# Block ring for u, joint turns, packed first values and a re-woven order in an attention-and-mixer kernel

## The chip, the core and the metric

The kernel runs on one core of one Trainium2 chip. The core has five engines, each with its own instruction queue: TensorE (PE: products, results in PSUM), VectorE (DVE), ScalarE (ACT), GpSimd (POOL, which also issues the loads that change the type) and SyncE (SP, which issues plain loads, the stores and the DMA transposes, here called turns). The metric is the time of one execution on the device, in microseconds. The kernel before takes 341.67 us, the median of 3 runs (340.97 to 342.67).

## The reference, cut to what matters

B = 8 batches, H = 8 heads, S = 576 tokens, 16 beacon keys, D = 64. Attention is causal over the tokens, and every token sees the beacons. Then come a low-rank mixing over tokens and a feed-forward part.

```python
scores = scale * np.matmul(q, k_all.transpose(0, 1, 3, 2))   # k_all: 16 beacons, then 576 tokens
scores = np.where(causal, -1000000000.0, scores)
a = np.exp(scores - scores.max(-1, keepdims=True)); a /= a.sum(-1, keepdims=True) + 1e-09
x = np.matmul(a, v_all)                                       # as (batch, token, 512)
h = x.transpose(0, 2, 1) @ U @ V                              # rank 32, over tokens
u = x + h.transpose(0, 2, 1)
out = u + np.maximum(u @ w_ch1, 0.0) @ w_ch2                  # 512 -> 2048 -> 512
```

## The kernel before

Attention works on pairs of heads, numbered 0 to 31: pair p is heads 2c and 2c + 1 of batch p // 4. Of a pair, q and k are loaded as rows, regrouped (`regroup`, tile `pr`) and turned into `qT` and `kT`. Pairs 0 to 11 are turned by PE products with the identity (`qkT_units`, tile `tps`); pairs 12 to 31 by a DMA transpose on SP (`turn_pair`, tile `raw`) and then put in token order by a copy (`order_units`). `score_units` makes the scores in four visits a to d (tile `sps`), each with two exponentials on ACT into `expt`; `mask_head` masks on DVE; `av_unit` multiplies with the values `vs`, in which column 65 of a head is one, and divides on DVE into `xb`.

Batch 0's q and k come as fp32 over SP and ACT's queues (`load_first`); every other load of q, k, v and the weights is on POOL's queue and changes to fp16 on the way. `v_loads` takes a beacon load and five loads of rows of 64 elements per batch or half batch.

`mix_units` makes u of a batch in a head and two parts of tokens, into `uT`, a ring of 3 x 512 tokens. For batches 0 to 2 x is brought in by products with the identity, from batch 3 on by turns of `xb` (`turn_x`, tile `xt`, one per 128 channels).

The feed-forward part works on nine blocks of 512 tokens of the flat batch-and-token axis (`block_steps`). For blocks 0 to 5, 16 units g make the hidden layer: four 512-column products each and the ReLU; for the lower half of the hidden layer the second 256 tokens are stored less the first 256, by one fused DVE instruction. Blocks 6 to 8 make the first layer by seven products F with sums (`first_product`, `first_sum`, `token_sum`). All blocks make the second layer by seven products P of sums (`operand_sum` p, `product`, `finish`), to which `finish` adds u, turned back to rows by SP (`turn`, tile `ut`, step U, one per 128 channels).

What sets the order is SCRIPT, a list of steps that is walked once: each step issues its instructions on its engines' queues, and each queue keeps that order. The letters: S a score visit, M a mask, A a product with values, G a regrouping, T a turned or reordered tile (with A, V or G for the engine ACT, DVE or POOL), R a DMA turn of a pair, X mixing, x a turn of x, k q b v loads, I a warm-up product, Z a tiny POOL copy that waits for a turn and so holds back the loads behind it. The tail after the bars is a guard on the sums of the softmax with a branch to a general path, which is not taken here.

Of the kernel before, what the change touches and what calls it, by code (L numbers as in the profile page):

```python
# [27 lines left out]
def kernel(  # L28
# [101 lines left out]
    Vsb = const.tile([P, S], F16, name="Vsb", tag="Vsb")  # L130
    ones = const.tile([P, 1], F16, name="ones", tag="ones")
# [4 lines left out]
    uT = const.tile([P, NCC, NBR * 512], F16, name="uT", tag="uT")  # L136
# [61 lines left out]
    def v_loads(src, bsrc, vs, hs):  # L198
        dst = vs[:, :].rearrange("p (c h e) -> p c h e", h=H, e=E)[:, :, hs, 0:D]
        beacon_load(nc.gpsimd, bsrc, dst[:, 0, :, :], hs)  # L200
        for j in range(NT):
            a = Nb if j == 0 else 0
            nc.gpsimd.dma_start(  # L203
                out=dst[a : a + nq[j], j, :, :], in_=src[hs, ds(q0[j], nq[j]), :].rearrange("h p d -> p h d")
            )

# [137 lines left out]
    def ring(t):  # L344

        return t % (NBR * 512)

    def turn_x(xb, xt, c):
# [3 lines left out]
            out=xt[:, c, :].rearrange("x (j p) -> x j p", p=P), in_=xb[:, c, :, :].rearrange("p j d -> p (j d)")  # L352
        )

    def mix_units(xb, u0, xt=None, shifted=True):
# [7 lines left out]
        edge = NBR * 512 - ring(u0)  # L363
        cuts = [0, edge if 64 <= edge < S else q0[2], S]
# [15 lines left out]
        def part(a, e):  # L380
            n = e - a
            ups = [pst([P, n], F32, name="ups") for _ in range(NCC)]
# [18 lines left out]
            for cc in range(NCC):  # L401
                dst = uT[:, cc, ds(ring(u0 + a), n)]
# [9 lines left out]
    def mlp_units(t0, n, dst):  # L412
# [4 lines left out]
        def g_unit(dc):  # L417
# [3 lines left out]
            for cc in range(NCC):  # L421
                nc.tensor.matmul(
                    g[:, 0:n], w1[:, cc, ts(dc, P)], uT[:, cc, ds(ring(t0), n)], start=(cc == 0), stop=(cc == NCC - 1)
# [8 lines left out]
        def c_unit(i, part):  # L432
# [10 lines left out]
            if part == 3:  # L443
                for cc in range(NCC):
                    nc.tensor.matmul(
                        ps[:m, ts(cc, P)], uT[:, cc, ds(ring(t0) + P * i, m)], ident, start=False, stop=True,
# [44 lines left out]
    def token_sum(t, i):  # L491

        H2 = 256
        x = uT[:, :, ds(ring(512 * t), 512)]
# [15 lines left out]
    def block_steps(t, dst):  # L510
# [6 lines left out]
        def turn(cc):  # L517
            if "u" not in cell:
                cell["u"] = utp.tile([P, 4, DM], F16, name="ut", tag="ut")
            nc.sync.dma_start_transpose(out=cell["u"][:, :, ts(cc, P)], in_=uT[:, cc, ds(ring(t0), 4 * P)])  # L520
            uses[t] += 1

        def g_unit(dc):
# [4 lines left out]
            for cc in range(NCC):  # L528
                nc.tensor.matmul(  # L529
                    g, w1[:, cc, ts(dc, P)], uT[:, cc, ds(ring(t0), 512)], start=(cc == 0), stop=(cc == NCC - 1)  # L530
                )
            if dc < NK:
                nc.scalar.activation(out=gT[:, dc, 0:H2], in_=g[:, 0:H2], func=AF.Relu)  # L533
                nc.vector.scalar_tensor_tensor(  # L534
                    out=gT[:, dc, H2:512], in0=g[:, H2:512], scalar=0.0, in1=gT[:, dc, 0:H2],
                    op0=ALU.max, op1=ALU.subtract,
                )
            else:
                nc.scalar.activation(out=gT[:, dc, :], in_=g, func=AF.Relu)  # L539
# [489 lines left out]
```

## Time and profile before

| | |
|---|---|
| median of 3 runs | 341.67 us |
| profiled execution | 341.91 us, span 340.3 us |
| busy: PE, DVE, ACT, POOL | 330.1, 263.4, 228.3, 103.6 us |
| granted TensorE clock, mean | 0.999 |
| chain that ended last | PE 84%, DVE 10%, issue 2%, ACT 1%, DMA 1% |
| DMA packets | 135600, 44.17 MB |

Busy times of engines overlap, so they don't add up to the span. A busy PE includes the warm-up products (tile `idle`, and some into `sps`): 44 of them in the first 36 us but for one. The chain is followed back from the last instruction; an engine's share of it says where the time went that nothing else hid. In a row of a group, the number behind the bar is the sum of busy us, then the mean ns of one instruction, then idle time of the engine just before it and who ended that. Line numbers are those of the kernel before.

### The profile page before, as it was taken

To read this page: it belongs to the slowest core of one execution; us is meant where nothing else is said; L and a number is where in the kernel's file an instruction comes from. 1 tells how busy PE (TensorE), PEld (TensorE's weight loads), DVE (VectorE), ACT (ScalarE), POOL (GpSimd) and SP (SyncE) were. 2 spreads that over 40 slices of the span, in tenths; PEclk is the share of its full clock that TensorE was granted. 3 is DMA by queue.
4 is the path that set the end of the run, shared out by engine and by line. 5 is a ranking of instruction groups with operands and counts; after the bars stand their busy time and mean duration, and the time that the engine had idled before them with its cause. 6 is when DMAs were issued, how large, how long until landed. Compare 5 with 4: busy or idle time off the path is not lost.

```text
span 340.3 us, 8963 instructions
## 1 busy us (share of the span) xinstructions
PE 330.1 (97%) x3527; PEld 227.9 (67%) x3527; DVE 263.4 (77%) x681; ACT 228.3 (67%) x495; POOL 103.6 (30%) x137
## 2 busy tenths in 40 slices
PE   6989999999999999999999999999999999999994
PEld 2456555684668755775577646765688888888883
DVE  3489687994869766984888768885999999896872
ACT  3779987849787889878886798267912842544500
POOL 7787673070530802360015220000001503303300
PEclk9999999999999999999999999999999999999999
DMA  8999999999999998999969998463445501203023
GB/s 170 237 188 167 126 184 197 118 127 213 159 163 189 163 203 127 128 148 191 183 95 145 175 174 115 33 161 99 48 63 159 85 13 63 77 3 94 3 80 128
DMA packets 135600, 44.17 MB, mean 130 GB/s; under 512 B 108384, under 2 KB 130912, under 8 KB 135552
## 3 DMA queue, kind: packets, MB, share of 16 engines
q0 software_dynamic: 69008, 17.54, 60.1%
q1 hardware_dynamic: 65952, 25.66, 39.9%
q8 instruction: 29, 0.48, 0.6%
q10 hardware_dynamic: 592, 0.34, 0.3%
q14 instruction: 19, 0.16, 0.2%
HBM read 37.63 MB, written 9.44 MB: 138 GB/s over the span
## 4 chain that ended last, share of the span: by engine, by line
PE 84%; DVE 10%; issue 2%; ACT 1%; DMA 1%; ACTq 0%; DVEq 0%
PE gps L529 25%; PE cpY L620 17%; PE cpD L620 9%; PE sps L316 8%; PE po L331 8%; PE cpA L620 4%; PE fpY L566 3%; DVE gT L581 3%; PE idle L241 2%; PE tps L263 2%; PE fpD L566 2%; DVE sT L601 1%; DVE ob L645 1%; DMA sth<-in_beacon_k_dram 1%; PE ups L397 1%
## 5 line engine op out<-in xcount | busy, mean ns | idle before, releaser
L321 ACT ACTIVATE expt<-sps 128x496 f16<-128x496 f32 (+2 forms) x256 | 111.6, 543 | 13.4 <-PE sps L316 11.9
L529 PE MATMUL gps<-uT,w 128*128 128x512 f16 x384 | 91.8, 380 | 0.0
L620 PEld LDWEIGHTS <-gT 128*128 128x128 f16 x576 | 54.6, 98 | 10.5 <-issue 2.3
L529 PEld LDWEIGHTS <-w 128*128 128x128 f16 x384 | 34.3, 98 | 37.1 <-issue 2.4
L587 POOL TENSOR_SCALAR gT<-gT 128x512 f16<-128x512 f16 x12 | 17.8, 1493 | 105.7 <-DVE gT L581 89.1
L620 PEld LDWEIGHTS <-sT 128*128 128x128 f16 x432 | 40.8, 98 | 8.0 <-issue 2.0
L203 POOL DMA_DIRECT2D vs<-in_v_dram x50 | 40.8, 838 | 3.8 <-DMA w<-in_moe_w_ch_dram 1.7
L304 DVE TENSOR_TENSOR expt<-expt,bigmask 128x512 f16<-128x512 f16 x64 | 26.9, 421 | 18.8 <-ACT expt L321 18.8
L331 PEld LDWEIGHTS <-expt 128*128 128x128 f16 (+1 forms) x960 | 35.2, 98 | 8.7 <-DVE expt L304 1.1
L539 ACT ACTIVATE gT<-gps 128x512 f16<-128x512 f32 x48 | 29.3, 618 | 15.4 <-PE gps L529 14.9
L331 PE MATMUL po<-vs,expt 128*128 128x65 f16 (+1 forms) x960 | 37.8, 194 | 0.7 <-DVE expt L304 0.6
L620 PE MATMUL cpY<-wsum,gT 128*128 128x256 f16 x288 | 36.1, 273 | 0.0
L620 PE MATMUL cpD<-w,sT 128*128 128x256 f16 x288 | 35.6, 273 | 0.3 <-DVE sT L601 0.3
L316 PE MATMUL sps<-qT,kT 64*128 64x80 f16 (+4 forms) x384 | 34.3, 284 | 0.2 <-DVE qT L265 0.2
L340 DVE TENSOR_TENSOR xb<-po,rec 128x320 f16<-128x320 f32 x64 | 31.5, 492 | 2.2
L534 DVE SCALAR_TENSOR_TENSOR gT<-gps,gT 128x256 f16<-128x256 f32 x48 | 19.7, 420 | 13.0 <-ACT gT L533 12.9
L109 ACT ACTIVATE hP<-fpY 128x512 f32<-128x512 f32 x24 | 13.7, 597 | 23.1 <-PE fpY L566 22.0
L533 ACT ACTIVATE gT<-gps 128x256 f16<-128x256 f32 x48 | 18.9, 412 | 12.2 <-PE gps L529 11.9
L316 PEld LDWEIGHTS <-kT 64*128 64x128 f16 x384 | 13.8, 94 | 19.8 <-issue 11.1
L645 DVE TENSOR_TENSOR ob<-cpY,ut 128x512 f32<-128x512 f32 (+1 forms) x28 | 18.7, 667 | 5.9 <-PE cpY L620 5.9
L566 PEld LDWEIGHTS <-wf 128*128 128x128 f16 x192 | 18.6, 98 | 3.1 <-issue 0.7
L620 PE MATMUL cpY<-w,gT 128*128 128x256 f16 x144 | 17.7, 273 | 0.0
(118 smaller groups left out, 484.7 us busy)
## 6 DMA issues: line engine op xcount, KB each, us to landing
out_dram<-ob SPq DMA_DIRECT2D x16, 512.0 KB, 4.7
st<-in_k_dram POOLq DMA_DIRECT2D x6, 512.0 KB, 8.0
st<-in_q_dram POOLq DMA_DIRECT2D x6, 512.0 KB, 8.3
vs<-in_v_dram POOLq DMA_DIRECT2D x18, 128.0 KB, 7.9
w<-in_moe_w_ch_dram POOLq DMA_DIRECT2D x4, 512.0 KB, 7.5
w<-in_moe_w_ch_dram POOLq DMA_DIRECT2D x2, 1024.0 KB, 12.0
stm<-in_k_dram SPq DMA_DIRECT2D x4, 256.0 KB, 6.0
out_dram<-ob SPq DMA_DIRECT2D x4, 256.0 KB, 2.8
```

The source lines that it names most:

```text
L203: nc.gpsimd.dma_start(out=dst[a : a + nq[j], j, :, :], in_=src[hs, ds(q0[j], nq[j]), :].rearrange("h p d -> p h d"))
L304: nc.vector.tensor_tensor(out=e4, in0=e4, in1=bigmask, op=ALU.min)
L316: nc.tensor.matmul(ps[i][:, ds(o, w)], kT[hp, c, ds(P * ch, P)], qT[hp, c, ds(qa, w)], start=True, stop=True,)
L321: nc.scalar.activation(out=ex[i][:, ds(PAD + SLOT * g, gw[g])], in_=ps[i][:, 0 : gw[g]], func=AF.Exp, scale=scale)
L331: nc.tensor.matmul(po[:, j, :], ex[0 : nk[c], ds(blk[(c, j)], P)], vs[0 : nk[c], ds(c * H * E + h * E, E)], start=(c == 0), stop=(c == j),)
L340: nc.vector.tensor_tensor(out=xb[:, h // 2, :, ds(D * (h % 2), D)], in0=po[:, :, 0:D], in1=r.broadcast_to([P, NT, D]), op=ALU.mult)
L529: nc.tensor.matmul(g, w1[:, cc, ts(dc, P)], uT[:, cc, ds(ring(t0), 512)], start=(cc == 0), stop=(cc == NCC - 1))
L534: nc.vector.scalar_tensor_tensor(out=gT[:, dc, H2:512], in0=g[:, H2:512], scalar=0.0, in1=gT[:, dc, 0:H2], op0=ALU.max, op1=ALU.subtract,)
L539: nc.scalar.activation(out=gT[:, dc, :], in_=g, func=AF.Relu)
L566: nc.tensor.matmul(ps[:, i, :], a[:, kk, ts(2 * mp + i, P)], b[:, kk, :], start=opens and i == 0 and kk == 0, stop=kk == 1, skip_group_che ...
L620: nc.tensor.matmul(ps[:, i, :], a[:, f, ds(P * i, P)], b[:, f, :], start=opens and i == 0 and f == 0, stop=f == NK - 1, skip_group_check=True,
L645: nc.vector.tensor_tensor(out=out, in0=ps[:, ii, :], in1=other, op=ALU.add)
```

## The change

1. `uT` is laid out by blocks: [P, 3, 4, 512] instead of [P, 4, 1536]. A batch's two parts of mixing are cut at the border of a block, 512 - 64 b tokens into batch b.
2. A turn of u and a turn of x take two groups of 128 channels each: 18 turns of u instead of 36, 10 of x instead of 20. `finish` reads the new layout of `ut`.
3. For blocks 0 to 5 the ReLU is one ACT instruction of full width; the difference of the token halves is taken in `operand_sum`, once per half of a block, for all nine blocks. The ReLU of 36 first products has a letter for its engine: 12 on POOL, 13 on DVE, 11 on ACT (before: 12 on POOL, 12 fused on DVE, 12 on ACT).
4. Batch 0's values are loaded with four tokens of a head in a row (tile `vf`, 116 partitions), and put in order by 16 products with a selection matrix `pick` (tile `vps`, steps D), copied to `vs` by ACT (2) and DVE (2).
5. SCRIPT is re-woven: 24 warm-up steps I instead of 37, 25 regroupings on POOL instead of 3, 20 of 40 reorderings of DMA-turned pairs on POOL instead of none.

```diff
-    uT = const.tile([P, NCC, NBR * 512], F16, name="uT", tag="uT")
+    uT = const.tile([P, NBR, NCC, 512], F16, name="uT", tag="uT")
...
+    def packed_loads(src, bsrc, vs, vf):
+        dst = vs[:, :].rearrange("p (c h e) -> p c h e", h=H, e=E)[:, 0, :, 0:D]
+        np_ = (S - nq[0]) // VJ
+        nc.gpsimd.dma_start(
+            out=vf[0:np_], in_=src[:, nq[0] : S, :].rearrange("h (p j) d -> p h (j d)", j=VJ)
+        )
+        nc.gpsimd.dma_start(out=dst[Nb : Nb + nq[0]], in_=src[:, 0 : nq[0], :].rearrange("h p d -> p h d"))
+        beacon_load(nc.gpsimd, bsrc, dst, ALLH)
+
+    def unpack(vf, vs, c, copy):
+        ps = pst([P, H, D], F32, name="vps")
+        n = nq[c]
+        rows = ds(VG * (c - 1), n // VJ)
+        for j in range(VJ):
+            nc.tensor.matmul(
+                ps[0:n], pick[rows, ds(VJ - 1 - j, n)], vf[rows, :, ds(D * j, D)], start=(j == 0), stop=(j == VJ - 1)
+            )
+        copy(out=vs[0:n, :].rearrange("p (c h e) -> p c h e", h=H, e=E)[:, c, :, 0:D], in_=ps[0:n])
...
-            out=xt[:, c, :].rearrange("x (j p) -> x j p", p=P), in_=xb[:, c, :, :].rearrange("p j d -> p (j d)")
+            out=xt[:, c : c + 2, :].rearrange("x c (j p) -> x (c j) p", p=P),
+            in_=xb[:, c : c + 2, :, :].rearrange("p c j d -> p (c j d)"),
...
-        edge = NBR * 512 - ring(u0)
-        cuts = [0, edge if 64 <= edge < S else q0[2], S]
+        cuts = [0, 512 - u0 % 512, S]
...
-            nc.sync.dma_start_transpose(out=cell["u"][:, :, ts(cc, P)], in_=uT[:, cc, ds(ring(t0), 4 * P)])
-            uses[t] += 1
+            nc.sync.dma_start_transpose(
+                out=cell["u"][:, cc : cc + 2, :, :].rearrange("x c j p -> x (c j) p"),
+                in_=ring(t0)[:, cc : cc + 2, :].rearrange("p c n -> p (c n)"),
+            )
+            uses[t] += 2
...
-            if dc < NK:
-                nc.scalar.activation(out=gT[:, dc, 0:H2], in_=g[:, 0:H2], func=AF.Relu)
-                nc.vector.scalar_tensor_tensor(
-                    out=gT[:, dc, H2:512], in0=g[:, H2:512], scalar=0.0, in1=gT[:, dc, 0:H2],
-                    op0=ALU.max, op1=ALU.subtract,
-                )
-            else:
-                nc.scalar.activation(out=gT[:, dc, :], in_=g, func=AF.Relu)
+            nc.scalar.activation(out=gT[:, dc, :], in_=g, func=AF.Relu)
...
-                if n == 3:
-                    nc.vector.scalar_tensor_tensor(
-                        out=n3, in0=n3, scalar=0.0, in1=a11, op0=ALU.max, op1=ALU.subtract
-                    )
-                elif n == 2:
-                    nc.gpsimd.tensor_scalar_max(out=out, in0=out, scalar1=0.0)
-                else:
-                    nc.scalar.activation(out=out, in_=out, func=AF.Relu)
+                RELU[eng](out)
...
+            if j == 0:
+                nc.vector.tensor_tensor(out=n3, in0=n3, in1=a11, op=ALU.subtract)
```

The order at three places. First ACT at the beginning, before; `sps` 225 and 226 are the two heads' scores of one visit, `st` is a tile of batch 1:

```order
L109 ACTIVATE pr<-stm 128x512
L109 ACTIVATE hd_142<-sth 80x128
L109 ACTIVATE qT<-tps 128x64
L109 ACTIVATE qT<-tps 128x512
L321 ACTIVATE expt_120<-sps_225 128x496
L321 ACTIVATE expt_121<-sps_226 128x496
L109 ACTIVATE pr<-st_191 128x512
L321 ACTIVATE expt_120<-sps_262 128x464
L321 ACTIVATE expt_121<-sps_263 128x464
L321 ACTIVATE expt_120<-sps_282 128x208
```

and after, from the first exponential on:

```order
L350 ACTIVATE expt_121<-sps_253 128x208
L350 ACTIVATE expt_122<-sps_254 128x208
L350 ACTIVATE expt_121<-sps_259 128x496
L350 ACTIVATE expt_122<-sps_260 128x496
L350 ACTIVATE expt_121<-sps_269 128x464
L350 ACTIVATE expt_122<-sps_270 128x464
L109 ACTIVATE kT_125<-tps 128x80
L109 ACTIVATE kT_125<-tps 128x512
L350 ACTIVATE expt_121<-sps_285 128x496
L350 ACTIVATE expt_122<-sps_286 128x496
L109 ACTIVATE vs_127<-vps 128x8x64
```

Three visits of pair 0 now follow each other, the regrouping of a later batch is gone from between them, and the unpacked values are copied here.

Second POOL at the beginning, before (`st` and `hd` are batch 1's k, `vs` batch 0's values):

```order
L196 DMA st_191<-in_k_dram 128x4x256
L190 DMA hd_189<-in_k_dram 64x4x64
L193 DMA hd_189<-in_beacon_k_dram 16x8x64
L193 DMA vs_126<-in_beacon_v_dram 16x4x64
L203 DMA vs_126<-in_v_dram 112x4x64
L203 DMA vs_126<-in_v_dram 128x4x64 x3
L203 DMA vs_126<-in_v_dram 80x4x64
L253 CAST pr<-stm 128x512
```

and after:

```order
L203 DMA hd_174<-in_beacon_k_dram 16x8x64
L220 DMA vf<-in_v_dram 116x8x256
L223 DMA vs_127<-in_v_dram 112x8x64
L203 DMA vs_127<-in_beacon_v_dram 16x8x64
L282 CAST pr<-stm 128x512
L780 CAST hd_142<-sth 80x128
L206 DMA st_177<-in_q_dram 128x4x256
L200 DMA hd_175<-in_q_dram 80x4x64
L206 DMA st_176<-in_k_dram 128x4x256
```

All of batch 0's values are now asked for ahead of batch 1's k and q, in three loads, where before one half came here and the other behind a slice of w1.

Third POOL in the middle, where batch 5's k is loaded, before (`gate` is the tiny copy of step Z):

```order
L196 DMA st_2119<-in_k_dram 128x8x256
L190 DMA hd_2117<-in_k_dram 64x8x64
L193 DMA hd_2554<-in_beacon_k_dram 16x8x64
L822 COPY gate_117<-raw 1x1
L196 DMA st_2557<-in_q_dram 128x8x256
L190 DMA hd_2555<-in_q_dram 80x8x64
```

and after:

```order
L865 COPY gate_118<-raw 1x1
L206 DMA st_2323<-in_k_dram 128x8x256
L200 DMA hd_2321<-in_k_dram 64x8x64
L206 DMA st_2324<-in_q_dram 128x8x256
L200 DMA hd_2322<-in_q_dram 80x8x64
L320 COPY qT<-raw 128x512 x2
L203 DMA hd_2321<-in_beacon_k_dram 16x8x64
L320 COPY kT_125<-raw 128x512
L865 COPY gate_118<-raw 1x1
L282 COPY pr<-st_2324 128x512
```

Before, only loads and the tiny copy stood here; now three reorderings of pairs 16 and 17 (`qT`, `kT`) and regroupings (`pr`) stand among the loads.

178 lines of the change are left out of this document (103 added, 75 removed).

## The prediction

> **What bounds the kernel now.** I read first the busy time by stretches, then the chain of work that ended last, then the instructions by group, and last the timeline of ScalarE (ACT) in the first 37 us. The stretches, with busy us and instructions per engine:
>
> ```profile
> 0.00:37.00 37.00, 32.53 (x356) 17.03 (x357) 24.17 (x95) 27.36 (x67) 27.80 (x51) 1.00 1.38 186
> 37.00:240.00 203.00, 202.97 (x2241) 130.48 (x2240) 155.50 (x426) 161.19 (x353) 58.03 (x74) 1.00 1.30 149
> 240.00:290.00 50.00, 49.19 (x525) 40.79 (x524) 47.83 (x103) 22.51 (x46) 8.98 (x6) 1.00 0.38 73
> ```
>
> The columns are PE, PE's weight loads, DVE, ACT, POOL, granted clock, DMA. After 37 us TensorE (PE) is busy without a hole for 203 us; in 240 to 290 DVE is nearly full too (47.83 of 50), and the chain runs there on DVE's sums; after that the chain is back on PE. Rows of the chain (start, us, what):
>
> ```profile
> 36.91 0.97 PE gps L529 x4
> ...
> 187.17 0.46 PE po L331 x15
> ...
> 195.42 3.45 PE gps L529 x16
> ...
> 269.95 2.50 DVE gT L581 x4
> ```
>
> Sixteen 512-column products in 3.45 us are 0.216 us each: in the dense part only fewer products or fewer seams between them could save anything, and the change removes no product. So there are three places to win or lose: the ramp up to the first feed-forward product at 36.91 us, the seams from 37 to 240, and the stage in which DVE is co-bound.
>
> **The ramp.** What holds it back is read on ACT, whose last bracket is its idle time before the row:
>
> ```profile
> 9.33 1.06 ACT L321 ACTIVATE expt<-sps 128x496 f16<-128x496 f32 x2 [1.09 <-PE sps L316]
> ...
> 11.71 1.00 ACT L321 ACTIVATE expt<-sps 128x464 f16<-128x464 f32 x2 [0.81 <-PE sps L316]
> 13.18 1.53 ACT L321 ACTIVATE expt<-sps 128x208 f16<-128x208 f32 x4 [0.46 <-PE sps L316]
> ...
> 25.30 1.06 ACT L321 ACTIVATE expt<-sps 128x496 f16<-128x496 f32 x2 [1.63 <-PE sps L316]
> ```
>
> ACT's work there, by the groups:
>
> ```profile
> L321 ACT ACTIVATE expt<-sps 128x496 f16<-128x496 f32 x128 | 68.1, 611 | 5.3 <-PE sps L316 4.6 <-ACT kT L109 0.6
> L321 ACT ACTIVATE expt<-sps 128x464 f16<-128x464 f32 x64 | 32.6, 577 | 3.6 <-PE sps L316 3.1 <-ACT gT L539 0.5
> L109 ACT ACTIVATE pr<-st 128x512 f16<-128x512 f16 x23 | 14.8, 652 | 4.3 <-DMA st<-in_k_dram 4.3
> L109 ACT ACTIVATE hP<-fpY 128x512 f32<-128x512 f32 x24 | 13.7, 597 | 23.1 <-PE fpY L566 22.0 <-ACT hP L109 0.7 <-DVE gT L581 0.2
> L109 ACT ACTIVATE kT<-tps 128x512 f16<-128x512 f16 x6 | 4.0, 664 | 0.0
> L109 ACT ACTIVATE kT<-tps 128x80 f16<-128x80 f16 x6 | 1.8, 296 | 1.0 <-PE tps L263 1.0
> L408 ACT ACTIVATE uT<-ups 128x336 f16<-128x336 f32 x4 | 1.6, 472 | 0.5 <-PE ups L397 0.5
> L109 ACT ACTIVATE Vsb<-vps 128x288 f16<-128x288 f32 x2 | 0.8, 532 | 0.0
> L408 ACT ACTIVATE uT<-ups 128x240 f16<-128x240 f32 x4 | 1.3, 368 | 0.0
> ```
>
> Up to the last write of u that the first product needs, ACT now has 42 exponentials, 5 turned pairs, 5 regroupings and a head copy, 2 spreads of V, 4 writes of u. After the change it has 44, 7, 2, none, none, 2, and 2 unpackings of values. Exponentials: four more of 464 and two fewer of 496, 4 x 0.577 - 2 x 0.611 = +1.09. Turns: 2 x (0.664 + 0.296) = +1.92. Regroupings: -3 x 0.652 = -1.96; the head copy counts as a 128x80 copy, -0.30. V: -1.06. Unpackings: 2 x 0.597 (the copy of as many fp32 elements out of PSUM) = +1.19. Writes of u: 2 x 0.597 - 2 x (0.472 + 0.368) = -0.49. Sum +0.4 us. DVE gives up three turns and takes two unpackings, the V spread and four small copies for the selection matrix; I count it as even. The unpacking's 16 products are 16 x 0.216 = 3.5 us of PE, and I cost them at nothing: PE is covered by its own warm-up products, of which the change drops 13 (13 x 0.216 = 2.8). If the cover is gone they cost up to 3.5.
>
> Against the +0.4 stand the waits. The first three rows wait because the four score groups of pair 0 are issued spread over other turns; afterwards three of them follow each other, so I take 1.4 of 1.09 + 0.81 + 0.46 = 2.36 us. The 1.63 at 25.30 I leave. Ramp: +0.4 - 1.4 = **-1.0**, bounds -3.6 (all four waits gone) and +3.9 (no wait gone, unpacking uncovered).
>
> **The loads of batch 0's values.** Twelve transfers become three. Landing times and the software queue as a whole:
>
> ```profile
> st<-in_k_dram POOLq DMA_DIRECT2D x6, 512.0 KB, 8.0
> vs<-in_v_dram POOLq DMA_DIRECT2D x18, 128.0 KB, 7.9
> ...
> q0 software_dynamic: 69008, 17.54, 60.1%
> ```
>
> Four times the bytes land in the same time when rows are long. The packed load has 116 x 8 x 256 x 2 bytes = 464 KB, so about 8 us after its issue at some 2.5 us: 10.5, when PE is at pair 0's scores. Counted at 0, since the unpacking stands behind those.
>
> **Joint turns.** 18 fewer turns of u and 10 of x.
>
> ```profile
> ut<-uT SPq DMA_TRANSPOSE x36, 3.8
> raw<-pr SPq DMA_TRANSPOSE x20, 4.6
> ...
> L520 SPq DMA_TRANSPOSE ut<-uT x36: 1189/1262/2685, 36.4 to 322.8; - x36
> ...
> L283 SPq DMA_TRANSPOSE raw<-pr x20: 1232/1266/3720, 83.0 to 223.4; - x20
> ```
>
> The turn raw<-pr already has eight 128-column blocks, as the joint turn of u will; u's has four now. Both hold SP 1.26 us, so the queue is freed of 28 x 1.26 = 35 us. Landing grows from 3.8 to 4.6; that of x, with ten blocks instead of five, to about 5 on the same slope. Who waits: the residual in `finish`, many products later, and the second part of a batch's mixing. For batch 7 six groups of eight and two of four 256-column products stand between the last turn of x and its use, 56 x 0.108 = 6.0 us, more than 5: cost 0, at worst the 5 - 3.8 = 1.2 once.
>
> **ReLU and differences.** For blocks 0 to 5 the half-width fused DVE instruction goes, ACT's ReLU is full width, and one bulk subtraction per half of a block comes:
>
> ```profile
> L534 DVE SCALAR_TENSOR_TENSOR gT<-gps,gT 128x256 f16<-128x256 f32 x48 | 19.7, 420 | 13.0 <-ACT gT L533 12.9
> L601 DVE TENSOR_TENSOR sT<-gT,sT 128x1024 f16<-128x1024 f16 x18 | 12.3, 683 | 0.2
> L583 DVE SCALAR_TENSOR_TENSOR gT<-gT 128x512 f16<-128x512 f16 x12 | 8.3, 692 | 1.5 <-DVE gT L581 0.5
> ...
> L533 ACT ACTIVATE gT<-gps 128x256 f16<-128x256 f32 x48 | 18.9, 412 | 12.2 <-PE gps L529 11.9
> L539 ACT ACTIVATE gT<-gps 128x512 f16<-128x512 f32 x48 | 29.3, 618 | 15.4 <-PE gps L529 14.9
> ```
>
> DVE: -19.7 + 12 x 0.683 = -11.5; ACT: 48 x 0.206 = +9.9. In blocks 6 to 8 DVE loses 12 x 0.692 = 8.3, gains 6 x 0.683 = 4.1 and 13 plain ReLUs; between the 0.335 and the 0.692 of the rows here and below that is 4.4 to 9, so about even in the co-bound stage. What DVE gains there is block 5's last fused instructions: half of 8 x 0.420 less 2 x 0.683, 1 us. I take **-0.5** for 240 to 290, bounds -2 and +1.
>
> **Work moved to POOL.** 20 of 40 reorderings of turned pairs and 22 more regroupings become POOL copies:
>
> ```profile
> L253 DVE COPY pr<-st 128x512 f16<-128x512 f16 x32 | 10.6, 335 | 0.0
> L291 DVE COPY kT<-raw 128x512 f16<-128x512 f16 x10 | 6.1, 606 | 0.8 <-DMA raw<-pr 0.8
> ...
> L587 POOL TENSOR_SCALAR gT<-gT 128x512 f16<-128x512 f16 x12 | 17.8, 1493 | 105.7 <-DVE gT L581 89.1 <-issue 16.5
> L196 POOL DMA_DIRECT2D st<-in_k_dram x8 | 7.1, 888 | 25.3 <-ACT kT L109 23.8 <-ACT expt L321 0.6 <-DMA w<-in_moe_w_ch_dram 0.5
> ...
> L190 POOL DMA_DIRECT2D hd<-in_k_dram x8 | 5.5, 684 | 0.0
> ...
> L253 POOL COPY pr<-st 128x512 f16<-128x512 f16 x1 | 0.6, 642 | 0.0
> ```
>
> POOL's reordering has no row. Its ends are 0.64 (the plain copy) and 1.49 (POOL's ReLU); scaled as DVE's, 0.642 x 606 / 335 = 1.16, which I take. ACT and DVE end some 5 and 15 us less loaded from 37 to 240, so that PSUM banks come free earlier and some seams close. No row prices a seam gone; the stretch's bounds are -3 and, POOL's copies late, +3. I take **-1.5**.
>
> Sum: 341.9 (the profiled execution; span 340.3, the rest lies around it; the median of the runs is 341.67) - 1.0 - 1.5 - 0.5, from the median: **338.7**.
>
> **Rivals.** (1) Nothing is gained: the exponentials and the loads set the ramp, PE's seams stay. ACT's sum of +0.4 speaks for it: 341.7. (2) More is gained, all waits of the ramp and both lower bounds in part: 335.5.
>
> (3) Slower: POOL is late. After the change the loads of batch 5's k and q stand on POOL, and behind them three reorderings and a beacon load, while PE has four g units, three groups of P and three A units to do before it needs pair 17: 4 x 0.864 + 3 x 0.864 + 3 x 0.46 = 7.4 us. The issues are 2 x (0.888 + 0.684) and at most 0.684 for the beacon, 3.8, so the copies may take 1.2 us each, hardly more than my 1.16. At 1.49 PE waits 0.9 us there; five such places give +4.5, less the gains: 345. A row shows how it could be worse:
>
> ```profile
> 5.77 0.23 DVE L741 CAST hd<-sth 80x128 f16<-80x128 f32 x1 [3.38 <-DMA sth<-in_beacon_k_dram]
> ...
> 20.53 1.16 DVE L741 CAST hd<-sth 80x128 f16<-80x128 f32 x1
> ```
>
> The same cast took 0.23 and 1.16 us, the second while POOL wrote a load of w1. The Trainium skill, SBUF — State Buffer, section "SBUF: two separate sides", says DVE and GpSimd share a port pair as an exclusive lock, held for a whole instruction; the trace agrees with it in that 0.9 us. By that rule 42 more POOL copies of 0.64 to 1.16 us could each hold up one DVE instruction, at an estimate some 20 us of DVE, which would eat the relief and make the seams' -1.5 a 0: 340.2.
>
> (4) Slower: the packed load runs on few DMA engines. All transfers of the trace have 128, 112, 80, 64, 32 or 16 partitions; this one has 116. A mean packet of the software queue is 0.601 x 340.3 x 16 / 69008 = 47 ns for 254 bytes; its 928 packets of 512 bytes are 47 to 94 ns. Over 16 engines that is 2.7 to 5.5 us, over four 11 to 22. In the second case it lands at 15 to 26 us instead of 10.5; PE stands in order at the unpacking, ACT has about 4 us of exponentials left: +3 to +10, 347. The Trainium skill, DMA: Bandwidth & Descriptors, section "Why a DMA increments its semaphore by 16 and not by 1", gives the rule: the largest divisor up to 16 of the slowest dimension, which for 116 is 4; and an exception in which the software queue uses ceil(partitions/16) per engine, 15 engines here. No run here shows which.
>
> **How the numbers follow.** Chances: forecast 0.40 (own range 336.5 to 340), more 0.12, nothing gained 0.22, POOL late 0.13, few engines 0.13. Half a per cent, 1.7 us, is about what a measurement of this kernel tells from no change. Faster: 0.12 and nearly all of 0.40, 0.50; same: 0.24; slower: 0.26. The range 334.5 to 345.5 leaves out half of the case of few engines and a tail below and above.
>
> **What would show it.** Right: the first feed-forward product at 35.5 to 36.5 us with ACT's early waits gone; the turn of u at 1.26 us on SP and 4.6 to landing; DVE some 15 us below 263; POOL's reordering near 1.1 us. Wrong: unpacking products that wait for the values' load, scores that wait for a POOL copy, or PE's stretch from the first product to the end not shorter than now.

## The result: slower by 5.6 %

The changed kernel takes 360.53 us, the median of 4 runs (359.48 to 361.86), against 341.32 us of the kernel before on the same chip (340.95 to 342.67). The ratio is 1.0557, with a 95 % interval of 1.0510 to 1.0604. The forecast was 338.7 with a range up to 345.5: wrong in sign and outside the range. A ratio leaves disturbed runs out (in experiment 1 the one of 351.09), so below it can differ from the quotient of the medians given beside it.

The profiled execution has a span of 358.7 us, 18.4 more than before. I read it in three stretches, by the first and the last start of the feed-forward products `gps` of blocks 0 to 5. Before, then after:

```profile
L529 PE MATMUL gps<-uT,w x384: 377/379/391, 36.8 to 242.1; 128*128 128x512 f16 x192
```

```profile
L563 PE MATMUL gps<-uT,w x384: 376/379/390, 49.8 to 260.4; 128*128 128x512 f16 x192
```

Up to the first product: 36.8 before, 49.8 after, +13.0. From the first to the last: 205.3 and 210.6, +5.3. From there to the end of the span: 98.2 and 98.3. So some 70 % of the loss is in the ramp, the rest in the middle, and the end is as long as it was.

**The ramp.** The tile of the packed values, with who waited for it, and how long its transfer took:

```profile
L231 PE MATMUL vps<-vf,pick x16: 577/626/645, 22.9 to 27.1; 32*128 32x512 f16 x12, 20*80 20x512 f16 x4
L220 POOL DMA_DIRECT2D vf<-in_v_dram x1: 1969/1969/1969, 2.6 to 2.6; - x1
...
  DVE vs L234: 13.7, 2
  ACT vs L109: 12.2, 2
  POOL hd L200: 12.1, 1
  PE vps L231: 10.2, 1
...
DMA to landing us min/median/max: 20.1/20.1/20.1
```

The load is issued at 2.6 us and its landing releases PE at 22.9, not at 10.5. PE, ACT, DVE and POOL all stand for it, between 10 and 14 us each. And the unpacking products take 577 to 645 ns each. By stretches (columns as in the prediction: PE, weight loads, DVE, ACT, POOL, clock, DMA share, GB/s):

```profile
12.00:15.00 3.00, 0.73 (x4) 0.10 (x2) 0.23 (x1) 2.14 (x6) 0.00 (x0) 1.00 1.36 215
15.00:18.00 3.00, 0.00 (x0) 0.00 (x0) 0.00 (x0) 0.00 (x0) 0.00 (x0) 0.55 1.34 227
18.00:21.00 3.00, 0.00 (x0) 0.00 (x0) 0.00 (x0) 0.00 (x0) 0.00 (x0) 0.50 1.12 153
...
26.00:30.00 4.00, 4.00 (x26) 1.74 (x23) 1.40 (x7) 2.47 (x6) 0.02 (x1) 0.50 1.02 144
30.00:35.00 5.00, 5.00 (x61) 2.98 (x59) 4.10 (x12) 3.26 (x9) 2.65 (x4) 0.76 0.28 34
```

None of these engines does anything from 15 to 21 us. The granted clock drops to one half while PE stands, and stays there until some way into 30 to 35 us, long after the work has come back: the shares of 0.55 and 0.76 put the drop at 15.3 us, 2.6 after PE's last product, and the return at 32.4. The Trainium skill, TensorE: Matmul & The Clock Gate, Part 1, puts that down to an activity window of about 3.4 us; the trace agrees as far as some three idle microseconds are enough to lose the clock, but here it took until past 30 us to get it back, over 9 us after PE had resumed.

**The middle.** The waits of PE:

```profile
PE vps L231 <- DMA vf<-in_v_dram: 10.2, 1, 10.2
PE po L360 <- DVE expt L333: 2.2, 4, 1.4
PE cpD L642 <- DVE sT L623: 1.8, 2, 1.6
```

Behind the load stand two waits for DVE, of 1.4 and 1.6 us at the longest. They end at 121.4 and 128.6 us. Ahead of the first, DVE and then POOL:

```profile
118.48 2.58 DVE L282 COPY pr<-st 128x512 f16<-128x512 f16 x1
120.98 0.41 DVE L333 TENSOR_TENSOR expt<-expt,bigmask 128x512 f16<-128x512 f16 x1
```

```profile
117.74 0.62 POOL L282 COPY pr<-st 128x512 f16<-128x512 f16 x1
118.29 1.07 POOL L320 COPY kT<-raw 128x512 f16<-128x512 f16 x1
119.30 1.05 POOL L320 COPY qT<-raw 128x512 f16<-128x512 f16 x1
120.30 0.60 POOL L282 COPY pr<-st 128x512 f16<-128x512 f16 x1
```

A DVE copy whose like takes 0.28 us lasts 2.58 us, as long as POOL copies one tile after another beside it. Ahead of the second, a sum that takes 0.68 us elsewhere takes 2.42 beside two more of POOL's copies:

```profile
126.14 2.42 DVE L623 TENSOR_TENSOR sT<-gT,sT 128x1024 f16<-128x1024 f16 x1
```

```profile
125.69 2.07 POOL L320 COPY qT<-raw 128x512 f16<-128x512 f16 x2
```

To compare kernels I use one sum below, DVE's *excess*: over all DVE instructions after 50 us that take over 0.1 us more than the median of their own line and shape, what they take above it. It is 1.2 us in 4 instructions before, 12.4 us in 20 after. By what POOL does beside them, some 9 of the 12.4 us stand beside its copies and some 3 beside its issues of loads; the 1.2 before stand mostly beside issues.

Some terms came out as forecast: POOL's reordering takes 1.10 to 1.14 us (estimate 1.16), and turns of x land in 5.0 (estimate 5).

### The profile page after: what moved, and what is told of

Its sections match the earlier page's. It is cut to its first block, busy times and chain, and to the rows that moved or that the text cites. A ratio compares the mean times of both kernels' runs of the same rounds, so it can differ in the third digit from the quotient of the medians.

```text
span 358.7 us, 8903 instructions
## 1 busy us (share of the span) xinstructions
PE 333.1 (93%) x3538; PEld 230.1 (64%) x3538; DVE 260.5 (73%) x640; ACT 220.5 (61%) x472; POOL 132.5 (37%) x171
## 4 chain that ended last, share of the span: by engine, by line
PE 68%; DVE 16%; ACT 6%; DMA 6%; issue 2%; POOL 0%; DVEq 0%; ACTq 0%; POOLq 0%
PE gps L563 17%; PE cpY L642 15%; PE cpD L642 9%; PE po L360 7%; DMA vf<-in_v_dram 6%; PE sps L345 5%; PE fpY L593 4%; ACT expt L350 4%; DVE sT L623 3%; PE cpA L642 3%; PE fpD L593 2%; ACT gT L566 2%; DVE xb L369 2%; DVE gT L608 2%; DVE expt L333 1%
## 5 line engine op out<-in xcount | busy, mean ns | idle before, releaser
L566 ACT ACTIVATE gT<-gps 128x512 f16<-128x512 f32 x96 | 56.0, 643 | 28.8 <-PE gps L563 28.2
L333 DVE TENSOR_TENSOR expt<-expt,bigmask 128x512 f16<-128x512 f16 x64 | 30.0, 469 | 25.7 <-ACT expt L350 25.6
L642 PEld LDWEIGHTS <-sT 128*128 128x128 f16 x432 | 41.0, 98 | 10.1 <-DVE sT L623 2.7
L213 POOL DMA_DIRECT2D vs<-in_v_dram x40 | 32.8, 833 | 4.3 <-DMA st<-in_k_dram 3.8
L282 POOL COPY pr<-st 128x512 f16<-128x512 f16 x22 | 14.1, 651 | 42.8 <-DMA raw<-pr 22.7
L345 PEld LDWEIGHTS <-kT 64*128 64x128 f16 x384 | 14.4, 96 | 20.1 <-issue 11.3
L320 POOL COPY qT<-raw 128x512 f16<-128x512 f16 x9 | 9.8, 1099 | 41.6 <-DMA raw<-pr 41.6
L320 POOL COPY kT<-raw 128x512 f16<-128x512 f16 x11 | 12.6, 1141 | 20.1 <-DMA raw<-pr 20.1
```

Source lines behind the costliest of these rows:

```text
L213: nc.gpsimd.dma_start(out=dst[a : a + nq[j], j, :, :], in_=src[hs, ds(q0[j], nq[j]), :].rearrange("h p d -> p h d"))
L320: copies[i](out=dst[:, c, w - 4 * P : w].rearrange("x (p j) -> x p j", j=4), in_=raw[:, i, :, :].rearrange("x j p -> x p j"),)
L333: nc.vector.tensor_tensor(out=e4, in0=e4, in1=bigmask, op=ALU.min)
L345: nc.tensor.matmul(ps[i][:, ds(o, w)], kT[hp, c, ds(P * ch, P)], qT[hp, c, ds(qa, w)], start=True, stop=True,)
L642: nc.tensor.matmul(ps[:, i, :], a[:, f, ds(P * i, P)], b[:, f, :], start=opens and i == 0 and f == 0, stop=f == NK - 1, skip_group_check=True,
```

## The experiments

Executions of the kernels that leave holes on PE scatter more than those of the kernel before (experiment 1 from 345.82 to 351.09 us, the kernel before beside it from 341.04 to 343.09). A hole may or may not cost clock: one of 2.0 us in experiment 12 is followed by 3.4 us at half clock, those of 1.4 and 1.6 us in the changed kernel's middle are not. Whether the scatter comes of that no run tests; I read the stretches beside the medians.

### 1. The packed load in two parts

```diff
-        np_ = (S - nq[0]) // VJ
-        nc.gpsimd.dma_start(
-            out=vf[0:np_], in_=src[:, nq[0] : S, :].rearrange("h (p j) d -> p h (j d)", j=VJ)
-        )
+        rest = src[:, nq[0] : S, :].rearrange("h (p j) d -> p h (j d)", j=VJ)
+        for p0, np_ in ((0, 112), (112, 4)):
+            nc.gpsimd.dma_start(out=vf[p0 : p0 + np_], in_=rest[p0 : p0 + np_])
```

> The changed kernel with its packed load of 116 partitions issued as two, of 112 and of 4 partitions; the same bytes to the same places, nothing else edited. Theory (few engines: with 116 partitions only four DMA engines carry the load, and everything queued behind it on those four waits too): the 112 partitions land at about 10 us instead of 22.7, PE's wait of 10.2 us at the unpacking goes, the granted clock stays 1.00, the first feed-forward product moves from 49.8 to about 37 us, and the time falls by about 13 to 347 (345 to 350), still above the kernel before. Rival (it is late by its amount or its place at the head of the queue): it lands after 18 us as now, and the time stays within 358 to 362.

Measured: 348.93 us (345.82 to 351.09), ratio 1.0133 (1.0088 to 1.0177). The two loads and the first product:

```profile
L230 PE MATMUL vps<-vf,pick x16: 372/374/406, 12.7 to 15.0; 32*128 32x512 f16 x12, 20*80 20x512 f16 x4
L221 POOL DMA_DIRECT2D vf<-in_v_dram x2: 601/720/840, 2.6 to 3.4; - x2
...
DMA to landing us min/median/max: 9.6/9.8/10.0
```

```profile
L562 PE MATMUL gps<-uT,w x384: 377/379/390, 38.2 to 250.3; 128*128 128x512 f16 x192
```

The first product starts at 38.2 instead of 49.8: 11.6 us are back, as many as the medians differ by (360.53 - 348.93 = 11.6). That these two agree so well is chance: the spans of the profiled executions differ by 10.1 us (358.7 and 348.6, the middle being 1.5 longer here), the ratios by 4.2 %, some 14 us. The rival that put the lateness down to amount or place falls, since both are unchanged. That it is the number of engines the trace shows in two more ways. The sixteen increments by which a load reports its parts done, for the 116-partition load and for the 112-partition one (us from the start):

```
116: 9.18 9.31 9.46 9.60 10.02 10.08 10.27 10.65 10.67 10.70 11.09 11.90 | 22.12 22.16 22.54 22.75
112: 8.07 8.13 8.17 8.71 8.83 9.03 9.04 9.24 9.27 9.29 9.30 10.24 10.40 11.62 12.02 12.59
```

I read this as twelve of sixteen engines with nothing to carry and four that carried it all. And the software queue's packets, after and in this run:

```profile
q0 software_dynamic: 68864, 17.55, 56.5%
```

```profile
q0 software_dynamic: 66192, 17.54, 56.8%
```

The same bytes in 2672 fewer packets. If four engines carry 116 x 8 / 4 = 232 packets each and every other engine runs through as many empty ones, that is 12 x 232 = 2784; less 12 x 8 for the four-partition load and 16 for the report of one load more, 2672 to the packet; the empty ones show as packets of 4 bytes, 2836 of them before 12 us after the change and 161 in this run.

### 2. Batch 0's values loaded as before

```diff
-    ... HqV0 I1 I1 f0 u ... Sa0:3 DA1 DV3 M0.1 q1A TqA1 I1 DA2 s DV4 Sc1 ... I1 w10 GqV5 ...
+    ... HqV0 I1 I1 v0A u ... Sa0:3 I4 I4 M0.1 q1A TqA1 I1 I4 s I4 Sc1 ... I1 w10 v0B GqV5 ...
```

> The changed kernel with batch 0's values loaded as before the change, in two halves by heads (the first at the place of the packed load, the second behind the load of w1's first quarter), and each of the four unpackings replaced by four warm-up products. Theory (few engines): time as with the packed load in two parts, 345 to 349, since both only take the late load away; first feed-forward product at 36 to 38 us. Rival (the re-woven order of the ramp is itself slow): the first feed-forward product stays beyond 42 us and the time above 352.

Measured: 350.38 us (348.16 to 351.23), ratio 1.0253 (1.0216 to 1.0290); first product at 40.7. Most of the lateness is gone here too, so the rival falls, but the time and the first product are both above what the theory said. By the ratios this kernel is over one per cent slower than experiment 1, and the intervals do not touch; the single times do overlap (348.16 to 351.23 against 345.82 to 351.09). Among PE's waits stands:

```profile
PE tps L292 <- POOL pr L282: 3.8, 1, 3.8
```

A regrouping that the new order gives to POOL stands behind the load issues of POOL's queue, of which there are twelve for batch 0's values instead of three. Under the new order the packed load is probably worth having, once it runs on all engines.

### 3. Warm-up products in the wait

```diff
-    ... Sa0:3 DA1 DV3 ...
+    ... Sa0:3 I48 DA1 DV3 ...
```

> The changed kernel with 48 more warm-up products of 512 columns (48 x 0.216 = 10.4 us) put ahead of the first unpacking on PE; their results are not used. They fill the wait for the load, which stays. Theory (the wait also costs clock: PE ran at half clock from 15.3 to 32.4 us because it stood still): granted clock 1.00 throughout, the 9.5 us of products done at half clock from 22.9 to 32.4 take 4.7, and the time falls by 3 to 5 us to 356 to 358. Rival (after the load has landed ACT and DVE set the pace of the ramp): within 1 us of 360.5 although the clock is 1.00.

Measured: 355.34 us (354.97 to 355.71), ratio 1.0390 (1.0350 to 1.0429). These are two runs, a gain of 5.2 us by the medians. The late load stays, the clock is 1.00:

```profile
12.00:23.00 11.00, 10.74 (x54) 4.77 (x53) 0.00 (x0) 2.11 (x6) 0.31 (x1) 1.00 1.10 168
23.00:33.00 10.00, 9.60 (x134) 5.58 (x130) 9.04 (x32) 9.03 (x24) 7.52 (x13) 1.00 0.95 134
```

```profile
L563 PE MATMUL gps<-uT,w x384: 376/379/390, 44.8 to 255.4; 128*128 128x512 f16 x192
```

The first product moves from 49.8 to 44.8: of the 11.6 us that the four engines cost, 5.0 are clock and 6.6 are waiting. Experiment 1's own ramp has 3.4 us at half clock, though; in experiments 4, 11 and 12, which have the same ramp, the clock stays whole and the first product comes at 36.6 to 36.8, by which the wait is 8 and the whole 13. DVE and ACT did not take up what the clock gave back; the rival falls.

### 4. POOL's copies given back to ACT and DVE

```diff
-    ... TkG13 ... TqG15 ... GkG18 ...
+    ... TkA13 ... TqV15 ... GkV18 ...   (all 20 reorderings, and the 16 regroupings of pairs from 12 on)
```

> As the kernel with the load in two parts, and besides all 20 reorderings of turned pairs that stood on POOL go back to ACT (11 of k) and DVE (9 of q), and the 16 regroupings of pairs from 12 on that stood on POOL go to DVE. Theory (a POOL copy holds up a DVE instruction for its whole length): DVE's single instructions of 2.58 us at 118.5 and 2.42 us at 126.1 take 0.28 and 0.68 again, PE's hole of 3.0 us between 120 and 140 closes, and the time falls by about 5 us against the kernel with the load in two parts, to 342 (340 to 344). Rival (the holes come of the order of the work or of the joint turns): the holes stay, and the time is within 1 us of the kernel with the load in two parts, or above it by the added work of ACT and DVE.

Measured: 366.88 us (364.70 to 367.77), ratio 1.0717 (1.0665 to 1.0770): 18 us slower than experiment 1 by the medians. Both expectations missed. DVE's excess did fall, from 12.0 to 3.2 us, but PE waits elsewhere:

```profile
PE gps L562 <- DVE uT L436: 9.0, 1, 9.0
PE po L359 <- DVE expt L332: 3.9, 1, 3.9
```

DVE stood still ahead of each:

```profile
138.36 0.50 DVE L281 COPY pr<-st 128x512 f16<-128x512 f16 x1 [9.74 <-DMA raw<-pr]
...
185.43 0.69 DVE L319 COPY qT<-raw 128x512 f16<-128x512 f16 x1 [4.41 <-DMA raw<-pr]
```

A regrouping has to wait until an earlier turn has read its buffer `pr`, a reordering until its turn has landed. In the changed kernel POOL spends 84 us on these two waits (22.7 for regroupings, 41.6 and 20.1 for reorderings of q and k), and PE's wait list shows 0.2 us behind it; on DVE, whose queue goes in order too, what PE needs next stands behind the wait. The order was written for POOL; this run doesn't price the hold-up.

### 5. Three of POOL's copies elsewhere

```diff
-    ... TkG14 ... TqG15 ... GkG18 ...
+    ... TkA14 ... TqA15 ... GkV18 ...
```

> The changed kernel with the load in two parts, and three of POOL's copies elsewhere: the reorderings of k of pair 14 and of q of pair 15 to ACT, the regrouping of k of pair 18 to DVE. In the kernel with the load in two parts POOL does these three in a row, and a DVE copy of 0.28 us that starts beside them at 107.2 us takes 3.5, while PE is busy only 16.98 of the 20 us from 100 to 120. Theory (the POOL copies hold DVE up, and that makes this hole): the DVE copy takes under 1 us, PE is busy over 19 of those 20 us, and the time falls by 2 to 5 us against the kernel with the load in two parts (348.9). Rival (ACT is full there, or what DVE does is not what PE waits for): the hole stays, time 347 to 351.

Measured: 349.10 us (346.93 to 351.40), ratio 1.0219 (1.0142 to 1.0295); the excess is 11.0 us. In experiment 1 there was

```profile
107.17 3.53 DVE L281 COPY pr<-st 128x512 f16<-128x512 f16 x1
```

Here the copy at 107 us takes 0.6 us and PE is busy 19.95 us from 100 to 120, as the theory has it; but from 120 to 140 it is busy only 17.41. DVE and POOL a little later:

```profile
115.28 2.45 DVE L334 TENSOR_TENSOR expt<-expt,mask 80x80 f16<-80x80 f16 x1
117.65 0.41 DVE L332 TENSOR_TENSOR expt<-expt,bigmask 128x512 f16<-128x512 f16 x1
```

```profile
115.58 2.08 POOL L319 COPY qT<-raw 128x512 f16<-128x512 f16 x2
```

A mask of 0.19 us takes 2.45, as long as the next two of POOL's copies. PE's holes from 120 to 140 are 0.92 and 0.22 us at 124.7, where experiment 4, without POOL's copies, has 0.93 and 0.21 before the same products, and 0.95 and 0.51 at 136.5, behind two masks that take 1.04 and 1.06 us beside a POOL copy. So the hold-up is real and moves to later copies, but only part of what PE loses here is its doing. The time stays where the rival had it.

### 6. The changed code under the old order

```diff
-    ... U0.0 ... U0.1 ... x12 ... x13 ... F62.3 F61.2 ... F63.3 ...
+    ... U0.0 ... x12 ... F62.3G F61.2 ... F63.3V ...   (order, loads and copies as before; each joint turn at its later place)
```

> The code of the changed kernel (ring of u by blocks, joint turns of u and x, full ReLU on ACT and differences in bulk) under the order of before: batch 0's values loaded as before, no unpacking, the copies on the engines that they had before; a joint turn stands where the later of its two single ones stood. Theory (these three parts cost nothing and gain little, the loss is the load and POOL): 340 to 342.5, POOL's part of DVE's delays gone. Rival (joint turns that land later, 4.2 and 5.0 us in place of 3.8 and 3.6, or the bulk difference ahead of the sums make PE wait): 343 to 347, with PE waiting on the second part of the mixing or on the sums of the cores.

Measured: 349.29 us (348.66 to 349.47), ratio 1.0219 (1.0170 to 1.0268). Both expectations are too low. POOL's part is gone as expected (excess 1.3 us), yet 7.5 us are lost: stretches of 36.9, 207.9 and 102.2 us against 36.8, 205.3 and 98.2.

### 7. POOL copies added to the kernel before

```diff
+        elif name == "J":
+            for i in range(2):
+                nc.gpsimd.tensor_copy(
+                    out=spare.rearrange("x (p j) -> x p j", j=2),
+                    in_=qT_of(int(arg) // NH2)[:, int(arg) % NH2, ds(S - 512 + 256 * i, 256)].rearrange(
+                        "x (j p) -> x p j", j=2
+                    ),
+                )
...
-    ... TqA12 ...
+    ... TqA12 J12 ...
```

> The kernel before with 40 POOL copies added, two behind each pair's reordering of q from pair 12 on, each from 256 columns of q in two-way order into a spare tile that nothing reads: no engine waits for them. Theory (a POOL copy holds up a DVE instruction that runs beside it, for its own length): DVE's time above the median of each instruction's own form after 50 us rises from 1.2 us to between 5 and 12, and the time by 1 to 4 us, to 343 to 346. Rival (the two engines do not disturb each other, and the long DVE instructions of the changed kernel come of something else): the excess stays below 2 us, and the time within 1 us of the kernel before.

Measured: 383.22 us (379.16 to 384.38), ratio 1.1181 (1.1092 to 1.1270). The excess is only 2.2 us, but:

```profile
PE po L332 <- DMA vs<-in_v_dram: 27.9, 14, 7.1
```

I had said that no engine waits for these copies. The loads behind them on POOL's queue do: a copy that waits for its q holds back the loads of later values, and PE stands for those. The run prices a mistake of mine, and shows how dear a POOL step is that waits.

### 8. POOL copies that wait for nothing

```diff
+        elif name == "J":
+            for i in range(int(arg)):
+                nc.gpsimd.tensor_copy(
+                    out=spare.rearrange("x (p j) -> x p j", j=2),
+                    in_=Vsb[:, ds(256 * (i % 2), 256)].rearrange("x (j p) -> x p j", j=2),
+                )
...
-    ... v3 ... q5 ...
+    ... v3 J4 ... q5 J4 ...   (behind 16 loads of later batches)
```

> The kernel before with 64 POOL copies of 256 columns in two-way order added, four in a row behind each of 16 loads of later batches, from the spread V (which is not written again) into a spare tile that nothing reads: unlike the copies of the earlier run they wait for nothing, so that no load is held behind one that waits. By that run's rows one takes 0.50 us, four some 2 us. Theory (while POOL's copies run in a row, a DVE instruction on half-precision data in SBUF waits for them): DVE's time above the median of each instruction's own form after 50 us rises from 1.2 us to between 5 and 15, and the time by 1 to 4 us, to 343 to 346. Rival (no such hold-up; the time of the earlier run came from the loads held behind the copies alone): excess below 2.5 us, time 341 to 342.5.

Measured: 343.50 us (342.99 to 345.11), ratio 1.0057 (1.0033 to 1.0080); excess 4.9 us in 20 instructions, against 1.2. So 64 copies make DVE 3.7 us longer and the kernel 1.7 to 2. This is the hold-up nearly by itself (the loads behind the copies start later too): real and small. The excess is just under the theory's 5, the time within its range. The single excesses are 0.14 to 0.27 us but for two of 0.41, which stand in the kernel before as well; all are less than one copy of 0.50. A DVE instruction got in between two of these copies. They write the same tile and stand 0.06 us apart in the trace, while the reorderings in a row start 0.05 to 0.08 us before the one ahead has ended; whether that is what makes the difference no run tried.

### 9. The same as 6, with ReLU and differences as before

```diff
-            nc.scalar.activation(out=gT[:, dc, :], in_=g, func=AF.Relu)
+            (ACT's half ReLU and DVE's fused instruction as before; no difference in operand_sum)
```

> The kernel with the changed code under the order of before, but with ReLU and differences as before: ACT's ReLU on half the columns and DVE's fused instruction for the other half, and DVE's fused difference in blocks 6 to 8. What is left of the change is the ring of u by blocks with the cuts of the mixing at its blocks, and the joint turns. Theory (the full ReLU on ACT and the differences in bulk cost the 7 us by which the changed code under the old order is slower): 341 to 343. Rival (the joint turns, which come later and land later, cost them): 346 to 350, with PE waiting behind the second parts of the mixing.

Measured: 343.79 us (343.07 to 344.86), ratio 1.0058 (1.0039 to 1.0077), between the two expectations. Ring, cuts and joint turns cost 0.6 %, 2.0 us; the other 5.5 us of experiment 6 are the full ReLU and the differences in bulk, under an order that does not fit them: 1.8 us in the middle (207.9 against 206.1) and 2.9 at the end (102.2 against 99.3). The ramps of the two profiled executions differ by 0.8 the other way.

### 10. Experiment 1 with the old ReLU in blocks 0 to 5

The `g_unit` of the kernel before, and the bulk difference only for blocks 6 to 8:

```diff
-            if j == 0:
+            if j == 0 and t > 5:
```

> The changed kernel with the load in two parts, and in blocks 0 to 5 ReLU and difference as before the change (ACT on half the columns, DVE's fused instruction on the other half; no bulk subtraction there). The order stays the re-woven one, with POOL's copies. Theory (ReLU and differences in bulk cost the stretch from the first to the last feed-forward product of blocks 0 to 5 some 2 us, as under the old order, where it went from 206.1 to 207.9): 345 to 347.5, that stretch 2 us or more shorter than the 212.1 of the kernel with the load in two parts. Rival (under the new order ACT has room for the full ReLU, and DVE, held up by POOL, has none for the fused instructions): 350 or more.

Measured: 354.93 us (351.93 to 356.40), ratio 1.0373 (1.0307 to 1.0440), 6 us slower than experiment 1 by the medians, 8 by the ratios; its middle stretch is 218.2 us instead of 212.1. The rival is right. Going back to the old ReLU gained 5.5 us under the old order and loses 6 here (in blocks 0 to 5 alone).

### 11. POOL's reorderings in halves

```diff
+            n = 2 if copies[i] == nc.gpsimd.tensor_copy else 1
+            m = P // n
+            for s in range(n):   (tokens ds(m * s, m) each)
```

> The changed kernel with the load in two parts, and each of POOL's 20 reorderings of a turned pair (1.1 us) cut into two copies of half the tokens. The same bytes, the same engines and order. Theory (DVE waits for the POOL copy that is running, and can start between two: beside copies of 0.50 us the longest excess was 0.25 to 0.27 us on the masks and sums): DVE's time above the median of its forms falls from 12.0 us to about half, no DVE instruction takes over 1.5 us, PE's hole of 3.0 us between 100 and 140 shrinks to under 1.5, and the time falls to 345 to 347. Rival (DVE waits until POOL pauses, however the copies are cut): single DVE instructions of 2 us and more stay, and so does the hole; time 347 to 350.

Measured: 347.71 us (346.44 to 348.62), ratio 1.0171 (1.0135 to 1.0207): not told apart from experiment 1. The excess falls to 8.9 us, less than hoped, and one DVE copy at 105.2 us still takes 2.4 us too long; PE is busy 17.57 of the 20 us from 100 to 120. At the place that matters DVE waited for the whole row of copies, however they were cut, as the rival had it.

### 12. Two reorderings on POOL exchanged

```diff
-    ... TkG15 X2.1 b6 GqG17 ... TkG14 Sc14 ...
+    ... TkG14 X2.1 b6 GqG17 ... TkG15 Sc14 ...
```

> The changed kernel with the load in two parts, and two reorderings on POOL exchanged in the order: that of k of pair 14 stands where that of pair 15 stood, and the other way round. In the kernel with the load in two parts POOL stands still for 3.72 us before 105.86, waiting for the turn of pair 15, with the reordering of pair 14 queued behind it; then four copies run in a row, PE waits 1.20 us for pair 14's k, and a DVE copy takes 3.53 us beside them, after which PE waits 1.43 us more. Theory (POOL's queue is late there, and its copies in a row hold DVE): both of PE's waits go or fall below 0.5 us, PE is busy over 19 of the 20 us from 100 to 120, and the time falls by 2 to 4 us, to 345 to 347. Rival (the hold-up comes again at the next run of POOL's copies, as where three copies were taken off POOL): PE's loss in 100 to 140 stays 2.5 us or more, time 347.5 to 350.

Measured: 347.10 us (345.18 to 348.52), ratio 1.0138 (1.0086 to 1.0191). Both aimed-at waits are gone, and in their place:

```profile
112.29 2.88 DVE L622 TENSOR_TENSOR sT<-gT,sT 128x1024 f16<-128x1024 f16 x1
```

```profile
112.55 2.06 POOL L319 COPY qT<-raw 128x512 f16<-128x512 f16 x2
114.53 0.54 POOL L203 DMA_DIRECT2D hd<-in_beacon_k_dram  x1
```

```profile
PE cpD L641 <- DVE sT L622: 2.0, 1, 2.0
```

PE loses 3.3 us from 100 to 140 (36.67 busy of 40), as the rival had it, though the time lies between the two expectations: the hold-up moves to a sum of 0.68 us, which takes 2.20 longer, about as long as two copies.

The kernels side by side, us (profiled executions):

| kernel | to the first product | first to last | to the end |
|---|---|---|---|
| before | 36.8 | 205.3 | 98.2 |
| after | 49.8 | 210.6 | 98.3 |
| 1 load in two parts | 38.2 | 212.1 | 98.3 |
| 2 old loads | 40.7 | 207.3 | 98.5 |
| 3 warm-up in the wait | 44.8 | 210.6 | 98.3 |
| 4 no POOL copies | 36.8 | 229.9 | 98.1 |
| 5 three copies off POOL | 38.7 | 208.6 | 99.2 |
| 6 old order | 36.9 | 207.9 | 102.2 |
| 7 before, waiting POOL copies | 36.2 | 247.0 | 98.4 |
| 8 before, free POOL copies | 35.9 | 207.5 | 98.2 |
| 9 old order, old ReLU | 37.7 | 206.1 | 99.3 |
| 10 as 1, old ReLU | 35.6 | 218.2 | 98.3 |
| 11 short POOL copies | 36.6 | 210.2 | 98.5 |
| 12 exchange | 36.8 | 210.4 | 98.3 |

No kernel here is faster than the one before.

## Why the prediction was wrong, point by point

**The packed load, "Counted at 0".** This is the step that failed. It took the landing of loads with other shapes, "about 8 us after its issue at some 2.5 us: 10.5", for one of 116 partitions. What happened is rival 4, to which I gave 0.13: four engines, landing at 22.7 inside its 15 to 26. Its price of 3 to 10 us was too small all the same: 11.6 by experiment 1 and more by others, since it counted the wait (6.6 to 8) and not the clock that PE loses while it stands (5.0, experiment 3). The rows said enough to give this rival more than 0.13: no transfer of the trace had such a shape, and on four engines the same packet times gave 11 us and more. The rule of the Trainium skill, DMA: Bandwidth & Descriptors, section "Why a DMA increments its semaphore by 16 and not by 1", the largest divisor up to 16, gives 4 for 116 and 16 for 112. Both agree with the increments; the exception that I set against it did not apply here.

**The ramp, -1.0.** With the load on all engines the first product is at 35.6 to 38.7 (experiments 1, 4, 5, 10, 11 and 12, which share this ramp) instead of 35.8. The kernel before has 36.8 and, with its ramp unchanged, 36.2 and 35.9 in experiments 7 and 8. All lie inside the bounds; a gain of 1.0 is not seen, but a single execution's ramp is too uncertain to exclude it. The unpacking's 3.5 us, counted at nothing, were not priced by any run; in experiment 1 PE waits 0.9 for the load ahead of them.

**The middle, -1.5.** It came out as +5.3 in the changed kernel between +4.9 and +6.8 in experiments 1, 11 and 12, and +2.0 and +3.3 in experiments 2 and 5. The bounds were -3 and +3. The reasoning was that ACT and DVE would end less loaded; DVE's busy time fell by 2.9 us only (263.4 to 260.5), not by some 15, because some 11 us of hold-up by POOL (12.4 - 1.2) took the place. A DVE instruction was held not for one POOL copy but through two to four in a row (2.45, 2.88, 2.58 and 3.53 us for instructions of 0.19, 0.68, 0.28 and 0.28). The rule of the Trainium skill, SBUF — State Buffer, section "SBUF: two separate sides", that DVE and GpSimd take a shared port pair as a lock, was set down as worth 1.5 us of lost gain. The rows agree with the lock, but the rule has it held for one instruction, and here DVE did not get in when the first one ended. Beside that, POOL's own lateness counts: rival 3 had it, at another place and with a smaller price. What the copies cost together with what they relieve can't be had from one run: taken off POOL they cost 18 us more under this order (experiment 4).

**Joint turns, 0.** They land about as estimated (4.2 and 5.0 us against 4.6 and 5), but hold SP longer than single ones, 1.55 and 1.66 us in the median instead of 1.26 and 1.30, so that SP's queue is freed of some 27 us and not of 35. Ring, cuts and turns cost 2.0 us under the old order (experiment 9). Which of the three it is, no run tells.

**ReLU and differences, -0.5.** The end took 98.3 instead of 98.2: nothing gained. Under the old order this part costs 5.5 us; under the new one it pays, since going back costs 6 us (experiment 10).

**The sum.** The four engines cost 11.6 us by the medians, which leaves 7.0 for the rest (348.93 - 341.91), and some 14 by the ratios, which leaves 1.3 % (0.9 to 1.8), some 4.5 us. Most of that rest is in the middle stretch. There PE's largest hole stands behind a DVE instruction held up by POOL in every kernel of the new order that keeps POOL's copies; how much of the 4.5 to 7 us is that, how much the 2.0 us of ring, cuts and turns and how much the order stays open, because each attempt to remove one hole opened the next.

## What to carry to other kernels

Before a load's shape is changed, look at its number of partitions: from 116 to 112 + 4 is 11.6 us or more here, and a late transfer at the head of an in-order queue costs twice, once as a wait and once as clock. Work moved to an idle engine is priced by what stands behind it on that engine's queue and by what runs beside it, not by the busy time it takes off the others. And a part of a change that was written together with an order can't be judged under another order: going back to the old ReLU was worth -5.5 us under one order and +6 or more under the other.

## What the runs showed of the hardware that I had not expected

- By the packet counts, the twelve engines without data are not idle: each runs through 232 packets of 4 bytes, as many as each of the four carries of 512. Loads queued behind also report twelve parts early and four late; the next one on the queue, with 112 partitions, has landed after 19.0 us.
- A DVE instruction on half-precision data in SBUF can be held for as long as POOL copies one tile after another: 3.53 us for a copy of 0.28 in experiment 1. Beside copies that wrote the same tile again and again the hold was 0.14 to 0.27 us. Why the two differ was not tried. POOL's issues of loads hold DVE too: in the kernel before a copy of 0.28 us takes 0.69 at 194.8 us beside two of them.
- In the changed kernel some three idle microseconds of PE took half the clock, and it was over 9 us of work until it was back. Shorter holes can cost clock too: 2.0 us were followed by 3.4 us at half clock in experiment 12.
